# Fast matrix products for five instead of four pairs in the second GEMM of an H3 + feed-forward kernel, with the factors of w2 made earlier and kept in DRAM

## The chip, the core and the metric

The kernel runs on one NeuronCore of a Trainium2 chip. The metric is the device time of one execution in microseconds (us), as the median of several runs. Engines: PE multiplies matrices, DVE (VectorE) and ACT (ScalarE) work element by element, POOL (GpSimd) here mostly issues DMAs, SP (SyncE) issues the other DMAs. Each engine runs its instructions in program order; they wait for each other by semaphores.

## The reference

x is [2048, 1024] (S by D), w1 [1024, 3584], w2 [3584, 1024] (D by F, F by D), all float32.

```python
xn = _layernorm(x, axis=-1)
return x + _A_ref(xn, A_k, A_v, A_shift_k, A_ssm_k, A_ssm_D) + _B_ref(xn, B_w1, B_w2)

def _A_ref(q, k, v, shift_k, ssm_k, ssm_D):   # H3
...
    kv = k_shift * v                          # k_shift: causal convolution of k, 4 taps
...
    y = irfft(rfft(kv, 2*S) * rfft(ssm_k, 2*S))[:S] + kv * ssm_D
    return q * y

def _B_ref(x, w1, w2):                        # feed-forward
    h = jnp.einsum("bsd,df->bsf", x, w1)
    h = _silu(h)
    return jnp.einsum("bsf,fd->bsd", h, w2)
```

(The two transforms along S are written shorter here.)

## The kernel before

Every matrix product is made of float16 pieces: a float32 operand is split into a high and a low half, and three matmuls (high by high, high by low, low by high) are summed in PSUM. A split is one ACT instruction (high) and one DVE scalar_tensor_tensor (low). Matmuls have 128x128 weights and as a rule 512 columns.

Stages, in the order of PE. **GEMM1** (`units()`, L1085; matmuls at L1027 to L1029) makes the activations h = silu(xn·w1), in 28 pairs i of two blocks j of 128 columns of F; much of it by seven products in the manner of Strassen (P1, P7, P6, P2, P5, P3, P4) instead of eight. The activations go to DRAM, `hs`. **GEMM2** (`feed_forward()`, L1134; matmuls at L1179 to L1181 in `steps2`) has two parts. The plain part runs over two halves of the columns of D (h), 16 row blocks (t) and five chunks (c) of four j: 20 of the 28 j. Then `units2()` (L1197) does the other eight j, the pairs in `PAIRS`, by the seven products, in eight units u of 7 products with one step per pair. For these pairs `quad` (L908) combines activations right after GEMM1's unit and stores them to DRAM, `hsfS` and `hsfA`. The w2 factors of the seven products (sums and differences of w2's quarters, split in halves) are made at the end of `norms_w2()` (L1388), from raw w2 loaded again, straight into SBUF, when the plain part frees the places for them. Split w2 chunks and these factors lie in eight large SBUF places (`x` tiles; `W2PLACE`, `FPLACE`).

Beside the GEMMs runs the **convolution** (`convolution()`, L1499), in eight groups of four t each: stage 1 of the transform on PE (L1668 to L1670), evacuated as `tmp` by DVE or `spec` by ACT, a pointwise part in `spec` on DVE and ACT, the inverse on PE (L1861 to L1863) from the split `zh`/`zl`, and `yt`, a DVE scalar_tensor_tensor that reads PSUM and is added to `out` in DRAM by POOL's DMAs. Stage 1 and inverse matmuls stand between the GEMMs' matmuls.

h tiles are loaded by `load_h()` (L1345) on SP, one DMA per tile (`wo<-hs`, and `wo<-hsfS`/`wo<-hsfA` for the products), into a ring of 12 halves of the six `wo` buffers. A half is free again after its last matmul, which sets how far ahead loads can go.

What sets the order: the kernel's Python program has a planner (`Order`, L107). Every part is a generator that yields operations; each engine's next instruction is the one whose estimated start less its stream's bias is smallest. Costs per operation are formulas (`V` for DVE, L320; `A` for ACT, L323; `T` for PE), biases are given with `add`. So a changed number moves instructions on every engine. All DVE tensor_tensor instructions are issued at L348, scalar_tensor_tensor at L351, ACT at L359, SP's DMAs at L332, transposing ones at L341, POOL's at L345.

Of the kernel before, what the change touches and what calls it, by code (L numbers as in the profile page):

```python
# [20 lines left out]
P = 128  # L21
# [9 lines left out]
W = 512  # L31
# [20 lines left out]
RAWS = {"B11": [(0, 0)], "B21": [(1, 0)], "B22": [(1, 1)], "T1": [(0, 1), (0, 0)], "T2": [(0, 0)],  # L52
        "T3": [(1, 1), (0, 1)], "T4": [(1, 0)]}
# [197 lines left out]

class Parts:
# [43 lines left out]
def h3_ffn_kernel(ctx, tc, x, kp, vs, fs, shift, dskip, w1, w2, cfwd, cinv, out):  # L296
# [53 lines left out]
    def v_stt(o, a, s, b, op0, op1, **k):  # L350
        return V(lambda: nc.vector.scalar_tensor_tensor(o, a, s, b, op0=op0, op1=op1), o,  # L351
                 [a, b] + ([] if isinstance(s, float) else [s]), **k)

    def a_act(o, i, func, scale=1.0, bias=None, total=None):
# [8 lines left out]
        p.busy += 0.07 * (len(ins) - 1) - 0.06 * (i.space == bass.MemoryType.PSUM)  # L363
        if total is not None:
            p.busy += 0.19
            p.writes.append(total)
# [11 lines left out]
    hsf = [{p[0]: dram.tile([4, P, NQ, 2, P], F16, name=f"hsf{p[0]}{b}") for p in PRODUCTS.values()} for b in range(2)]  # L378
# [111 lines left out]
    def norm_act(ring, ss, ns, then, flags, margin=1.5, joined=False):  # L490
# [15 lines left out]
        yield V(chain, e, [sums], us=0.33)  # L506
# [293 lines left out]
    def scales_w1():  # L800
        for n, (_, i) in enumerate(pairs):
            yield (0.25, 0.2, 0.1, 0.05)[min(n, 3)]
# [105 lines left out]
    def quad(i, sp):  # L908

        def factors(names, hf, toks=()):  # L910
# [4 lines left out]
            for f, name in enumerate(names):  # L915
                yield L(hsf[sp][name][:, :, PAIRS.index(i)].rearrange("q p h s -> p q (h s)"),
                        ht[:, 4 * f:4 * f + 4].rearrange("p q h s -> p q (h s)"))
                ttok.set()
# [103 lines left out]
    def steps(o, w, xf, first, last, more=False):  # L1022

        for k in range(KH):
# [5 lines left out]
            yield T(mm, o, [w[:, :, k], xf[:, :, k]], 3 * (size(o) / 2400 + 0.003))  # L1030
# [54 lines left out]
    def units():  # L1085
# [5 lines left out]
        for n, (i, sp) in enumerate(todo):  # L1091
# [3 lines left out]
            if i in PAIRS:  # L1095
                add(quad(i, sp), 0.1)
# [37 lines left out]
    def feed_forward():  # L1134
# [12 lines left out]
        for h in range(2):  # L1147
            for ts in TOGETHER[h]:
                pos = {}
                for c in range(NC):  # L1150
                    for t in ts:
# [7 lines left out]
                        yield from steps2(pos[t][0], hx, wc, c == 0, c == NC - 1)  # L1159
# [3 lines left out]
                        if c == NC - 1:  # L1163
                            add(result(h, t, *pos[t]), EB)
                            if h == 0:
                                flag["result", t].set()
        flag["last part"].set()
# [6 lines left out]
    def steps2(po, hx, wc, first, last, more=False, of=range(4), q=slice(0, W)):  # L1174
        o = po[:, q]
        for n in of:
            def mm(n=n):
                kw = dict(skip_group_check=more)
                nc.tensor.matmul(o, hx[:, n, 0, :], wc[:, n, 0, q], start=first and n == 0, stop=False, **kw)  # L1179
                nc.tensor.matmul(o, hx[:, n, 0, :], wc[:, n, 1, q], start=False, stop=False, **kw)  # L1180
                nc.tensor.matmul(o, hx[:, n, 1, :], wc[:, n, 0, q], start=False, stop=last and n == 3, **kw)  # L1181
            yield T(mm, o, [hx[:, n], wc[:, n, :, q]], 3 * (size(o) / 2400 + 0.005))
# [14 lines left out]
    def units2():  # L1197

        def product2(n, u, o, first=False, of=range(4), q=slice(0, W)):
# [4 lines left out]
            yield from steps2(o, hx, wc, first, True, not first, of, q)  # L1204
            if 3 not in of or q.stop < W:
                return
            htok.set()
            if u == len(tiles2) - 1:
# [5 lines left out]
        for u in range(len(tiles2)):  # L1214
# [18 lines left out]
            if last:  # L1233
                yield from product2("P2", u, one[0], of=(0, 1))
# [6 lines left out]
            if last:  # L1241
                yield from product2("P2", u, one[0], of=(2, 3))
# [102 lines left out]
    def load_h():  # L1345
        yield flag["factors"]
        for h in range(2):
            for c, t in [(c, t) for ts in TOGETHER[h] for c in range(NC) for t in ts]:
                yield wo.ready
                flag["h", h, t, c].what = o, _ = wo.tile([P, 4, 2, P], F16)  # L1350
                yield L(o, hs[t // 4][t % 4][:, PLAIN[4 * c]:PLAIN[4 * c] + 4])
                flag["h", h, t, c].set()
        for u, n in uses2():
            sp, q = tiles2[u]
            yield wo.ready
            flag["h2", u, n].what = o, _ = wo.tile([P, NQ, 2, P], F16)
            yield L(o, hsf[sp][PRODUCTS[n][0]][q])
            flag["h2", u, n].set()
        flag["h end"].set()
# [28 lines left out]
    def norms_w2():  # L1388
# [17 lines left out]
        add(load_w2(), 0.05)  # L1406
        for h in range(2):
            for c in range(NC):
# [5 lines left out]
                flag["w2", h, c].n = 2  # L1414
                for a in (0, 2):
                    i = PLAIN[4 * c + a] // 2
                    raw, tok = yield from next_w2()
                    add(split(wc[:, a:a + 2, 0, :], wc[:, a:a + 2, 1, :], raw, tau[:, i:i + 1], (tok, flag["w2", h, c])), 0.05)
        yield places[FPLACE[0]].ready
        hold, ktok = places[FPLACE[0]].tile([P, NQ, W], F32)  # L1420
        for k, (name, (_, of)) in enumerate(PRODUCTS.items()):
            r = places[FPLACE[k + 1]]
            yield r.ready
            wc, wtok = w2f[name] = r.tile([P, NQ, 2, W], F16)
            flag["w2f", name].n = NQ
            held = of in ("T2", "T3", "T4")
            if held:
                if of != "T3":
                    yield flag["held", before]
                flag["held", of].n = NQ  # L1430
                before = of
            for a, i in enumerate(PAIRS):
                raw, tok = yield from next_w2()
                src, toks = raw, (tok, flag["w2f", name])
                if held:
                    src, toks = hold[:, a], (flag["w2f", name], flag["held", of])
                if of == "T3":
                    b12, t12 = yield from next_w2()
# [566 lines left out]
```

## Time and profile before

| | |
|---|---|
| time of 3 runs, median (lowest to highest) | 1239.55 us (1238.06 to 1240.69) |
| span of the profiled execution | 1235.0 us (its own total time is not recorded) |
| busy: PE, DVE, ACT, POOL | 1225.7, 1121.9, 744.0, 142.0 us |
| DMA traffic | 293.21 MB, mean 237 GB/s |

The page gives busy time per engine, then a chain of work that ended last; the views of the trace add waits (who waited for whom, total us, times, longest), groups by line and shape (busy us, mean ns), windows (busy us and count per engine in a stretch) and a timeline. A mean in a group is the time from an instruction's start to its end; neighbours on an engine overlap a little, so that starts can lie closer.

GEMM1's last matmul starts at 580.8 us, the last load for the plain part of GEMM2 is issued at 1033.4 us, and the last matmul of all starts at 1230.3 us.

### The profile page before, as it was taken

Reading aid. Unit: us, or ns where it says so; the run is one execution under the profiler, and the core shown is the slowest. Engines: PE = TensorE matmul, PEld = TensorE weight load, DVE = VectorE, ACT = ScalarE, POOL = GpSimd, SP = SyncE. Lnnn points to the kernel's source line nnn. Section 1 sums busy time; section 2 is a strip of 40 time slices with the busy share of each in tenths; the row PEclk is TensorE's granted clock in tenths of the full one; section 3 lists DMA queues with packets and bytes.
Section 4 is the critical chain, followed back from the end, with each engine's and each line's share of the span. In section 5 each row is a group of like instructions: output and inputs, shape, how many; then the busy total and the mean of one; then the engine's idle time right before and its main releaser. Section 6 shows DMA issues by size and latency. Waiting matters only on the chain.

```text
span 1235.0 us, 17269 instructions
## 1 busy us (share of the span) xinstructions
PE 1225.7 (99%) x6128; PEld 596.6 (48%) x6128; DVE 1121.9 (91%) x1366; ACT 744.0 (60%) x1299; POOL 142.0 (12%) x164
## 2 busy tenths in 40 slices
PE   9999999999999999999999999999999999999998
PEld 7645444444444444444444544544454454445445
DVE  8999996989699979998999899989979979998993
ACT  7778887877767787758653632563263264536231
POOL 2000000000000020001110300210030030113114
PEclk9999999999999999999999999999999999999999
DMA  9289889999999698968997887699596688978777
GB/s 341 78 278 312 304 298 308 286 273 335 324 359 286 218 303 278 268 213 242 345 336 184 190 257 179 155 271 259 115 216 171 134 167 247 255 161 137 164 147 103
DMA packets 254438, 293.21 MB, mean 237 GB/s; under 512 B 48784, under 2 KB 167824, under 8 KB 252176
## 3 DMA queue, kind: packets, MB, share of 16 engines
q1 hardware_dynamic: 227760, 267.46, 69.3%
q0 software_dynamic: 26592, 24.65, 15.1%
q8 instruction: 48, 0.79, 0.3%
q14 instruction: 38, 0.31, 0.1%
HBM read 193.48 MB, written 98.57 MB: 236 GB/s over the span
## 4 chain that ended last, share of the span: by engine, by line
PE 96%; DVE 2%; ACT 1%; issue 1%; DMA 1%; POOL 0%; DVEq 0%
PE ff L1179 15%; PE ff L1180 15%; PE ff L1181 15%; PE ff L1027 13%; PE ff L1028 13%; PE ff L1029 13%; PE ps L1668 2%; PE ps L1669 2%; PE ps L1670 2%; PE ft L616 1%; PE ps L1863 1%; PE ps L1861 1%; PE ps L1862 1%; DMA out<-yt 1%; PE ff L1932 1%
## 5 line engine op out<-in xcount | busy, mean ns | idle before, releaser
L1180 PE MATMUL ff<-x,wo 128*128 128x512 f16 (+2 forms) x872 | 328.5, 377 | 0.0
L1179 PE MATMUL ff<-x,wo 128*128 128x512 f16 (+2 forms) x872 | 328.4, 377 | 0.0
L1181 PE MATMUL ff<-x,wo 128*128 128x512 f16 (+2 forms) x872 | 328.4, 377 | 0.0
L1028 PE MATMUL ff<-x,wo 128*128 128x512 f16 (+2 forms) x840 | 306.7, 367 | 1.5 <-DVE x L351 1.5
L1027 PE MATMUL ff<-x,wo 128*128 128x512 f16 (+2 forms) x840 | 306.7, 367 | 0.2 <-ACT hf L359 0.2
L1029 PE MATMUL ff<-x,wo 128*128 128x512 f16 (+2 forms) x840 | 306.7, 367 | 0.1
L348 DVE TENSOR_TENSOR spec<-spec 128x1024 f32<-128x1024 f32 (+2 forms) x272 | 263.0, 999 | 2.4
L1181 PEld LDWEIGHTS <-wo 128*128 128x128 f16 x872 | 85.3, 98 | 101.5
L1179 PEld LDWEIGHTS <-wo 128*128 128x128 f16 x872 | 85.3, 98 | 100.7
L1180 PEld LDWEIGHTS <-wo 128*128 128x128 f16 x872 | 85.3, 98 | 99.4
L1029 PEld LDWEIGHTS <-wo 128*128 128x128 f16 x840 | 82.1, 98 | 92.3 <-issue 1.6
L1027 PEld LDWEIGHTS <-wo 128*128 128x128 f16 x840 | 82.1, 98 | 88.1
L1028 PEld LDWEIGHTS <-wo 128*128 128x128 f16 x840 | 82.1, 98 | 86.9 <-issue 0.5
L345 POOL DMA_DIRECT2D out<-hf x59 | 52.5, 890 | 445.0 <-ACT hf L359 341.8
L359 ACT ACTIVATE hf<-ff,invc 128x512 f32<-128x512 f32 x60 | 41.0, 684 | 101.4 <-PE ff L1181 81.8
L345 POOL DMA_DIRECT2D out<-yt x56 | 62.0, 1278 | 326.4 <-DVE yt L351 186.7
L348 DVE TENSOR_TENSOR tmp<-spec 128x2048 f32<-128x2048 f32 (+1 forms) x48 | 92.3, 1932 | 0.9
L351 DVE SCALAR_TENSOR_TENSOR ht<-hf,wsc,ht 128x1024 f16<-128x1024 f32 (+1 forms) x56 | 67.4, 1203 | 14.5 <-ACT ht L359 14.0
L351 DVE SCALAR_TENSOR_TENSOR acc<-kin,taps,acc 128x1024 f32<-128x1024 f32 x48 | 61.4, 1278 | 7.3 <-ACT acc L359 7.3
L359 ACT ACTIVATE spec<-ps 128x512 f32<-128x512 f32 x96 | 55.4, 591 | 19.9 <-PE ps L1670 18.6
L359 ACT ACTIVATE spec<-spec 128x1024 bf16<-128x1024 f32 x32 | 33.7, 1054 | 54.9 <-DVE spec L348 54.9
L351 DVE SCALAR_TENSOR_TENSOR wo<-raw,wsc,wo 128x512 f16<-128x512 f32 (+1 forms) x56 | 56.4, 1011 | 8.3 <-ACT wo L359 8.1
(183 smaller groups left out, 1751.1 us busy)
## 6 DMA issues: line engine op xcount, KB each, us to landing
wo<-hs SPq DMA_DIRECT2D x160, 256.0 KB, 3.6
hs<-ht SPq DMA_DIRECT2D x80, 256.0 KB, 4.5
wraw<-in_w SPq DMA_DIRECT2D x31, 512.0 KB, 5.4
out<-hf POOLq DMA_DIRECT2D x59, 256.0 KB, 4.5
raw<-in_w SPq DMA_DIRECT2D x28, 512.0 KB, 5.8
kin<-in_kp SPq DMA_DIRECT2D x16, 704.0 KB, 6.2
kf<-in_fs SPq DMA_DIRECT2D x8, 1024.0 KB, 5.9
hl<-in_vs SPq DMA_DIRECT2D x32, 256.0 KB, 6.1
```

Source lines behind the costliest of these rows:

```text
L345: return Op("POOL", 1.1, 4.8, lambda: nc.gpsimd.dma_start(o, i, accum_op=ADD), [i], [o], m, n)
L348: return V(lambda: nc.vector.tensor_tensor(o, a, b, op=op), o, [a, b], **k)
L351: return V(lambda: nc.vector.scalar_tensor_tensor(o, a, s, b, op0=op0, op1=op1), o, [a, b] + ([] if isinstance(s, float) else [s]), **k)
L359: nc.scalar.activation(o, i, func, scale=scale, **kw)
L1027: nc.tensor.matmul(o, w[:, 0, k], xf[:, :, k, 0], start=first and k == 0, stop=False, **kw)
L1028: nc.tensor.matmul(o, w[:, 0, k], xf[:, :, k, 1], start=False, stop=False, **kw)
L1029: nc.tensor.matmul(o, w[:, 1, k], xf[:, :, k, 0], start=False, stop=last and k == KH - 1, **kw)
L1179: nc.tensor.matmul(o, hx[:, n, 0, :], wc[:, n, 0, q], start=first and n == 0, stop=False, **kw)
L1180: nc.tensor.matmul(o, hx[:, n, 0, :], wc[:, n, 1, q], start=False, stop=False, **kw)
L1181: nc.tensor.matmul(o, hx[:, n, 1, :], wc[:, n, 0, q], start=False, stop=last and n == 3, **kw)
L1668: nc.tensor.matmul(o, cf[:, 0], hi[i], start=i == 0, stop=False, **kw)
L1669: nc.tensor.matmul(o, cf[:, 0], lo[i], start=False, stop=False, **kw)
```

## The change

The change has five parts. (1) Pair 7 joins the four pairs done by the seven products (`MORE`), so the plain part has 18 j in chunks of 4, 4, 4, 2 and 4. Its activations go to DRAM tensors of their own (`hsx`), four and three products to a tensor, and one load (`wo<-hsx`) brings a batch for a unit. (2) The factors of w2 are made by `factors_w2` while the plain part runs: each pair's raw rows are loaded once (two DMAs of 512 KB), split into a pair of `wo` halves lent for it (`Lent`), and stored to DRAM (`w2s`); `load_w2f` loads them into the places later, pair 7's apart (`HOMES`). Two more `wo` tiles go to these for good, so 7 halves stay for the h tiles. (3) `load_w2` waits for a flag before loading into places used a second time. (4) The planner's costs of DVE, ACT and PE operations are other numbers. (5) So are some biases.

```diff
-PAIRS = (8, 9, 12, 13)
-NQ = len(PAIRS)
-PLAIN = [j for j in range(NF) if j // 2 not in PAIRS]
-NC = len(PLAIN) // 4
+MAIN = (8, 9, 12, 13)
+MORE = (7,)
+PAIRS = MAIN + MORE
+NM, NE, NQ = len(MAIN), len(MORE), len(PAIRS)
+CHUNKS = [(0, 4), (4, 4), (8, 4), (12, 2), (20, 4)]
+NC = len(CHUNKS)
-FPLACE = (6, 3, 4, 0, 1, 5, 2, 7)
+FPLACE = (3, 4, 0, 1, 5, 2, 7)
+HOMES = ((6, 4), ("wo", 2), ("wo", 1))
...
-        return Op("DVE", us or 1.03 * (size(o) / 960 + 0.075), 0.16, f, ins, [o], m)
+        return Op("DVE", us or size(o) / 960 + 0.072, 0.16, f, ins, [o], m)
-        return Op("ACT", us or 1.02 * (0.16 + size(o) * 0.84e-3), 0.2, f, ins, [o], m)
+        return Op("ACT", us or 0.1 + size(o) / 1200, 0.2, f, ins, [o], m)
...
+        p.busy += 0.0 if isinstance(s, float) else 0.06
...
-            yield T(mm, o, [hx[:, n], wc[:, n, :, q]], 3 * (size(o) / 2400 + 0.005))
+            yield T(mm, o, [hx, wc[:, :, q]], 3 * (size(o) / 2400 + 0.0024))
...
     def load_h():
         yield flag["factors"]
+        yield wo.pairs
+        whole, _ = wo.pair([P, 2 * W])
+        ctxs["stage"] = Lent([whole])
+        for where, n in HOMES:
+            if where == "wo":
+                yield wo.ready if n * NE == 1 else wo.pairs
+                t, _ = (wo.tile if n * NE == 1 else wo.pair)([P, n, NE, 2, W], F16)
+                lent.append(t)
...
             yield L(o, hsf[sp][PRODUCTS[n][0]][q])
             flag["h2", u, n].set()
+            k, f = BATCH[n]
+            if f == 0:
+                m = min(NX, 7 - NX * k)
+                yield wo.ready
+                o, tok = wo.tile([P, NX, NE, 2, P], F16, m)
+                flag["h2x", u, k].what = o, tok
+                yield L(o[:, 0:m], hsx[sp][k][q])
+                flag["h2x", u, k].set()
...
+    def factors_w2():
...
+        def factors(names, src, i, tok):
+            n = len(names)
+            stage = ctxs["stage"]
+            yield stage.ready if n == 1 else stage.pairs
+            o, otok = (stage.tile if n == 1 else stage.pair)([P, n, 2, W], F16, n)
+            yield from split(o[:, :, 0], o[:, :, 1], src, tau2[:, i:i + 1], (tok,))
+            for f, name in enumerate(names):
+                n = product_of[name]
+                yield L(w2s[n][:, PAIRS.index(i)], o[:, f])
+                otok.set()
+                flag["w2s", n].set()
+
+        for i in PAIRS:
...
+                yield L(r, w2r[:, 2 * i + q].rearrange("p (h w) -> p h w", h=2))
...
+            yield from factors(("B21", "B22"), low, i, ltok)
+            yield v_tt(low[:, 1], low[:, 1], top[:, 1], SUB)
+            yield v_tt(top[:, 1], top[:, 1], top[:, 0], SUB)
+            yield from factors(("B11", "T1"), top, i, ttok)
+            yield v_tt(top[:, 0], low[:, 1], top[:, 0], ADD)
+            yield v_tt(low[:, 0], low[:, 0], top[:, 0], SUB)
+            add(factors(("T4", "T3"), low, i, ltok), SB)
+            add(factors(("T2",), top[:, 0:1], i, ttok), SB)
...
+    def load_w2f():
...
+        for k, name in enumerate(PRODUCTS):
+            yield flag["w2s", name]
+            r = places[FPLACE[k]]
+            yield lambda: r.ready() and flag["w2 last", FPLACE[k]]()
+            wc, wtok = w2f[name] = r.tile([P, NM, 2, W], F16)
+            yield L(wc, w2s[name][:, 0:NM])
+            flag["w2f", name].set()
+            if not left:
+                left = yield from home(*homes.pop(0))
+            w2x[name] = left.pop(0)
+            yield L(w2x[name], w2s[name][:, NM:])
...
-        for gen, bias in ((loads(), 0.05), (load_v(), 0.04), (gate(), 0.04), (signal_parts(), CB), (parts_of(), CB), (stage1(), 0.02),
-                          (transforms(), 0.02), (squares_w2(), 0.0), (rest(floor), 0.0)):
+        for gen, bias in ((loads(), 0.05), (load_v(), 0.14), (gate(), 0.04), (signal_parts(), CB), (parts_of(), CB), (stage1(), 0.02),
+                          (transforms(), 0.0), (squares_w2(), 0.0), (rest(floor), 0.0)):
...
-    add(spill_w1(), 0.0)
+    add(spill_w1(), 0.2)
...
-    add(load_h(), 0.05)
+    add(load_h(), 0.3)
```

How instructions move is best seen in three places. The first is DVE in the plain part of GEMM2, at the last two yt of the convolution's group 3 (line L351 before is L364 of the change, L348 is L361). Before:

```order
L351 SCALAR_TENSOR_TENSOR zl1_6998<-spec_2120,csc1_5560,zh1_6997 128x1024
L348 TENSOR_TENSOR tmp_6880<-tmp_6880,ps2_6881 128x2x256
L348 TENSOR_TENSOR tmp_6880<-tmp_6880,ps3_6885 128x2x256
L351 SCALAR_TENSOR_TENSOR hl0_2121<-kf_6275,csc0_6397,hl0_2121 128x512
L351 SCALAR_TENSOR_TENSOR yt0_3150<-ps1_6999,csc1_5560,ht1_200 128x512
L351 SCALAR_TENSOR_TENSOR zl0_7045<-spec_2120,csc1_5560,zh0_7044 128x1024
L348 TENSOR_TENSOR tmp_6880<-tmp_6880,ps0_7019 128x2x256
L351 SCALAR_TENSOR_TENSOR yt0_3150<-ps3_7043,csc1_5560,ht1_200 128x512
```

The change, at the same yt:

```order
L364 SCALAR_TENSOR_TENSOR zl1_7243<-spec_2184,csc1_5505,zh1_7242 128x1024
L361 TENSOR_TENSOR spec_2184<-spec_2184 128x2x512
L364 SCALAR_TENSOR_TENSOR wo0_201<-wraw0_3215,tau2_166,wo0_201 128x2x512
L361 TENSOR_TENSOR tmp_7088<-tmp_7088,ps3_7089 128x2x256
L361 TENSOR_TENSOR tmp_7088<-tmp_7088,ps0_7093 128x2x256
L361 TENSOR_TENSOR wraw0_3215<-hf1_208,wraw0_3215 128x512
L361 TENSOR_TENSOR hf1_208<-hf1_208,wraw0_3215 128x512
L364 SCALAR_TENSOR_TENSOR hl1_2186<-kf_6390,csc0_6513,hl1_2186 128x512
L364 SCALAR_TENSOR_TENSOR yt0_3214<-ps2_7244,csc1_5505,ht1_211 128x512
L364 SCALAR_TENSOR_TENSOR zl0_7304<-spec_2184,csc1_5505,zh0_7303 128x1024
```

Between the same parts of the convolution now stand splits of w2 factors (into `wo0_201`, the lent buffer) and the sums of raw quarters (`wraw`, `hf`) that make them.

The second place is SP's queue in the plain part, late, where the first two factors (products P1 and P7) are stored for the last pair and loaded back:

```order
L345 DMA wo_202<-hs_84 128x512
L354 DMA_TRANSPOSE hl_2186<-cm 128x8x128
L345 DMA w2sP_77<-wo_201 128x1024
L345 DMA w2sP_81<-wo_201 128x1024
L345 DMA x_7293<-w2sP_77 128x4096
L345 DMA x_7307<-w2sP_77 128x1024
L345 DMA kf<-in_fs 128x2048
L345 DMA ht_211<-in_x 128x2x128 x2
L345 DMA w2sP_83<-wo_201 128x1024
L345 DMA w2sP_78<-wo_201 128x1024
L345 DMA x_7392<-w2sP_78 128x4096
L345 DMA x_7307<-w2sP_78 128x1024
```

None of these stores and reloads exists before; each reload waits for the store just ahead of it, and the h loads (`wo<-hs`) stand behind it in the queue. The 128x512 load is the chunk of two j.

The third place is the end of SP's queue. Before:

```order
L332 DMA wo_193<-hsfA_69 128x1024
L332 DMA wo_190<-hsfS_70 128x1024
L332 DMA wo_190<-hsfS_71 128x1024
L332 DMA wo_191<-hsfA_72 128x1024
L332 DMA hf_197<-out 128x512 x2
L332 DMA out<-hf_197 128x512
```

The change:

```order
L345 DMA wo_202<-hsfA_69 128x1024
L345 DMA wo_202<-hsfS_70 128x1024
L345 DMA hf_209<-out 128x512 x2
L345 DMA wo_204<-hsx_76 128x768
L345 DMA wo_205<-hsfS_71 128x1024
L345 DMA wo_206<-hsfA_72 128x1024
L345 DMA out<-hf_209 128x512
```

The load of `out`, which waits for the convolution's last yt to be added, was behind all h loads and now stands ahead of three.

More of the change, by code (lines that the diff above doesn't have):

```diff
@@ L249, in pair, with __init__ @@
         return shaped(self.taken(k), shape, dt), token
+class Lent(Halves):
+    def __init__(self, whole):
+        self.whole = whole
+        self.held = [[None, None] for _ in whole]
+        self.age = [0] * len(whole)
+        self.count = 0
 class Parts:
```

177 lines of the change are left out of this document (98 added, 79 removed).

## The prediction

> **What bounds the kernel now.** I read the page first: the busy shares, then the chain that ended last.
>
> ```profile
> span 1235.0 us, 17269 instructions
> ...
> PE 1225.7 (99%) x6128; PEld 596.6 (48%) x6128; DVE 1121.9 (91%) x1366; ACT 744.0 (60%) x1299; POOL 142.0 (12%) x164
> ...
> PE 96%; DVE 2%; ACT 1%; issue 1%; DMA 1%; POOL 0%; DVEq 0%
> ```
>
> PE is busy for 99% of the span and is 96% of the chain, so a matmul that goes is a matmul's time won, as long as what feeds PE keeps up. Next, the waits of PE over the whole run:
>
> ```profile
> PE ff L1028 <- DVE x L351: 1.5, 1, 1.5
> PE ps L1668 <- DVE yt L351: 1.4, 1, 1.4
> PE ff L1932 <- DVE oneb L402: 1.1, 1, 1.1
> PE ps L1668 <- DVE tmp L348: 0.5, 1, 0.5
> PE ff L1027 <- ACT hf L359: 0.2, 1, 0.2
> ```
>
> The 1.5 and 1.1 belong to the first 20 us, which the change leaves alone. The other three are 2.1 us, all between 569 and 588 us, where GEMM1 ends. Two of them are waits for DVE, the second engine at 91%. So the third view is that of windows, over the end of GEMM1 and the plain part of GEMM2 (busy us and instructions of PE, PEld, DVE, ACT, POOL; clock; DMA share; GB/s):
>
> ```profile
> 550.00:600.00 50.00, 47.88 (x245) 23.75 (x243) 45.66 (x52) 37.96 (x53) 7.57 (x8) 1.00 0.91 253
> 600.00:650.00 50.00, 50.00 (x234) 22.70 (x233) 49.79 (x50) 28.94 (x55) 5.59 (x6) 1.00 1.06 342
> 650.00:700.00 50.00, 50.00 (x258) 24.99 (x257) 48.00 (x54) 24.82 (x47) 7.42 (x8) 1.00 0.79 189
> 700.00:750.00 50.00, 50.00 (x235) 22.66 (x233) 45.18 (x47) 22.23 (x49) 8.33 (x9) 1.00 0.88 229
> 750.00:800.00 50.00, 50.00 (x257) 24.90 (x256) 46.17 (x53) 20.21 (x37) 7.38 (x8) 1.00 0.72 163
> 800.00:850.00 50.00, 50.00 (x233) 22.63 (x233) 45.59 (x52) 29.54 (x57) 7.49 (x8) 1.00 0.98 277
> ```
>
> PE has no gap from 600 us on, and DVE idles 0.2 + 2.0 + 4.8 + 3.8 + 4.4 = 15.2 us of these last 250. This idle time is the room into which the change puts work.
>
> **Fewer matmuls.** The plain part has 18 j instead of 20: 2 j × 16 t × 2 halves × 3 matmuls = 192 fewer. The products have five pairs instead of four: 8 units × 7 products × 1 pair × 3 = 168 more. Net 24 fewer; the program order confirms it, 866 instead of 872 on each of GEMM2's lines plus the same narrow pieces at the end. What one costs is its distance to the next, not its 379 ns:
>
> ```profile
> 1150.12 0.38 PE L1180 MATMUL ff<-x,wo 128*128 128x512 f16 x1
> ...
> 1166.09 0.38 PE L1179 MATMUL ff<-x,wo 128*128 128x512 f16 x1
> ```
>
> These two starts are 74 matmuls apart: 15.97 / 74 = 0.216 us. 24 × 0.2156 = **5.17 us** less PE work. Nothing else on PE changes in amount.
>
> **More work on DVE and ACT, at another time.** The rows that price it:
>
> ```profile
> L351 DVE SCALAR_TENSOR_TENSOR ht<-hf,wsc,ht 128x1024 f16<-128x1024 f32 x48 | 61.4, 1279 | 10.9 <-ACT ht L359 10.4 <-DMA kin<-in_kp 0.3
> L348 DVE TENSOR_TENSOR hf<-ff,hf 128x512 f32<-128x512 f32 x52 | 35.6, 684 | 3.7 <-PE ff L1029 3.7
> L351 DVE SCALAR_TENSOR_TENSOR x<-x,tau,x 128x512 f16<-128x512 f32 x12 | 8.8, 742 | 0.0
> L359 ACT ACTIVATE ht<-hf,wsc 128x1024 f16<-128x1024 f32 x48 | 54.9, 1145 | 1.2 <-DVE hf L348 0.2
> L359 ACT ACTIVATE x<-x,tau 128x512 f16<-128x512 f32 x12 | 8.5, 719 | 19.1 <-DVE x L348 19.1
> ```
>
> Pair 7's activations add 2 splits of 1024, 2 of 512 and 8 sums of 512; the w2 factors go from 20 splits of 1024, 28 of 512 and 16 sums to 33, 5 and 20. Together +15 × 1.279 − 21 × 0.742 + 12 × 0.684 = +11.8 us on DVE and +15 × 1.145 − 21 × 0.719 = +2.1 us on ACT. ACT, busy at 60%, hides its share. DVE goes to about 1133.7 of some 1230 us, still not the bound of the run; but the work now stands between about 600 and 800 us, and the burst after 1000 us shrinks.
>
> For that stretch I sum DVE's work in program order against PE's. A row's own duration is too long for this, since neighbours overlap:
>
> ```profile
> 569.44 1.28 DVE L351 SCALAR_TENSOR_TENSOR x<-wraw,tau,x 128x1024 f16<-128x1024 f32 x1
> 570.64 1.28 DVE L351 SCALAR_TENSOR_TENSOR ht<-x,wsc,ht 128x1024 f16<-128x1024 f32 x1
> 571.84 0.69 DVE L348 TENSOR_TENSOR hf<-ff,hf 128x512 f32<-128x512 f32 x1
> ```
>
> Two 1.28 us splits start 1.20 us apart; 512-wide sums likewise cost 0.60 to 0.65, 512-wide splits 0.665. From GEMM1's end to the last yt of the convolution's group 3 (its fourth), before has 219 DVE instructions, 206.9 us, against 216.4 us of matmuls. Of the change I count 42 more: 17 splits of 1024 (20.4 us), 20 sums of 512 (12.4), four spec sums of 1024 (4.7), and small ones: 245.4 us against 234.5 us of matmuls. DVE falls behind PE. The place that decides is shortly ahead: a yt that frees PSUM for a stage-1 matmul has 236.9 us of DVE work before it and 234.5 on PE's side, a wait of 2.4 us near 810 us. I checked the method on before: there the same sum's only shortfall is 0.56 us, at a stage-1 matmul, and the trace has this at that place:
>
> ```profile
> 569.58 0.38 PE L1668 MATMUL ps<-hl,cfw 128*128 128x512 f16 x1 [0.54 <-DVE tmp L348]
> ```
>
> On before the sum runs 0.6% longer than the trace, so of the 2.4 us I take off 1.4 and keep 1.0. The other shortfalls of the change, at matmul positions 228, 411, 552 and 898 us, are 0.1, 0.7, 1.1 and 1.5 us, with the same correction 0.1, 0.1, 0.4 and 0.1. Before lost 2.1 us in three waits where its sum has 0.56, so I add 0.6 us of hand-over for each of the last three places (552, 810, 898), and 0.7 us for late loads (next part): 1.7 + 1.8 + 0.7 = **4.2 us** of stalls past the start. The bounds: 0, if DVE always runs ahead of its order, and the full idle time of the windows (rival C).
>
> **Shorter load distance.** The lent wo pair and the places for w2's pair 7 leave 7 halves instead of 12 for the h tiles. Loads are then issued 54 to 72 matmuls ahead (11.6 to 15.5 us; 45, 9.7 us, at the least, in the products) instead of some 130 (28 us). Rows on what a load takes, in 560 to 620 us, in 620 to 622, and in the products (count, size, median us to landing):
>
> ```profile
> wo<-hs SPq DMA_DIRECT2D x18, 256.0 KB, 6.5
> ...
> wo<-hs SPq DMA_DIRECT2D x1, 256.0 KB, 9.8
> ...
> wo<-hsfS SPq DMA_DIRECT2D x32, 256.0 KB, 3.3
> ```
>
> In the products 9.7 against 3.3 is safe. At 580 to 640 us, with 342 GB/s and a DMA share of 1.06, the longest landing leaves 11.6 − 9.8 = 1.8 us for SP's own issuing; I take 0.7 us of loss in all, between 0 and rival D. The 18 MB of factor stores and reloads run after 625 us, where the windows have 163 to 277 GB/s. In two places SP's queue holds a reload behind the store just issued; the h loads queued behind it, and through them PE, have about 9 us left there, against a landing of 3 to 5.
>
> Two small edits cost nothing. Stage 1's PSUM halves get 9 other matmuls in between (1.94 us) instead of 12, and ACT's copy needs 0.59:
>
> ```profile
> L359 ACT ACTIVATE spec<-ps 128x512 f32<-128x512 f32 x96 | 55.4, 591 | 19.9 <-PE ps L1670 18.6
> ```
>
> At the end the hf<-out load, which in before sits on SP until the last yt is out, now stands ahead of the last three wo loads:
>
> ```profile
> 1194.57 21.64 SPq L332 DMA_DIRECT2D hf<-out  x2
> ...
> 1215.60 0.74 DVE L351 SCALAR_TENSOR_TENSOR wo<-ps,csc,ht 128x512 f32<-128x512 f32 x1
> ...
> 1228.69 2.67 SPq L332 DMA_DIRECT2D out<-hf  x3
> ```
>
> That would starve PE if the yt came as late as 1215.6; but the change has the fourth t's yt ahead of the last unit's sums, so SP should be free some 20 us before the end, and the first of the three loads is needed 9 us before it: 6 us to spare after its landing. The tail behind the last matmul stays.
>
> **The sum.** The profiled span of 1235.0 us lies 4.55 us under the median of 1239.55; I carry that over. 1239.55 − 5.17 − 2.1 (stalls that were) + 4.2 (stalls to come) = **1236.5 us**. Within 0.2% (2.5 us) is what a measurement here can't tell from no change: faster means below 1237.1, slower above 1242.0.
>
> **The rivals.**
> - **B, given back.** DVE keeps a third of its 15.2 us of idle time, 5.1, in the stretch to 810 us, because part of it is waits inside one chain: 1236.5 + 5.1 − 2.4 (what the freed order still absorbs between 810 and 898) = 1239.2. For it: the waits of DVE in 600 to 810 us, below, are mostly for ACT. Against it: a DVE that is late finds its inputs ready.
> - **C, DVE becomes the bound.** All of the idle time up to 810 us stays, 0.2 + 2.0 + 4.8 + 3.8 + about 0.9 = 11.7 us; stage 1 at 810 us then waits for yt by 11.7 + 1.0: 1239.55 − 5.17 − 2.1 + 12.7 = 1245.0. It decides from 8.8 us of kept idle time on (slower), 6.3 breaks even.
>
> ```profile
> DVE spec L348 <- ACT spec L359: 4.7, 4, 3.5
> DVE acc L351 <- ACT acc L359: 3.3, 1, 3.3
> DVE tmp L348 <- ACT spec L359: 2.0, 4, 0.6
> ```
>
> - **D, the ring of 7 halves starves PE** at 580 to 640 us. If a load takes longer than its 11.6 us from freed half to landed tile, each turn of the ring (about 11 us) loses the excess, some 6 turns there: 1.5 us too long (11.6 of landing and 1.5 of issuing) costs 9 us, 1236.5 − 0.7 + 9 = 1244.8. For it: 9.8 us landings. Against: the median of 6.5.
> [...]
>
> **How the numbers follow.** Forecast 0.48 (faster, 1233.6 to 1237.1), B 0.31 and E 0.02 (within 0.2%), C 0.10 and D 0.09 (slower). So faster 0.48, same 0.33, slower 0.19. The range leaves out the better part of C and D (0.15) and, below, 0.04 for a run that loses no time at all (1239.55 − 5.17 − 2.1 = 1232.3): 1233.6 to 1243.
>
> **What would show it.** PE's busy time falls by about 5 us, and 24 matmuls are gone from GEMM2's lines. DVE is busy for over 49 of 50 us in each window from 600 to 800 us, with its waits for ACT spec nearly gone there. PE's waits name DVE yt or tmp at a stage-1 line near 800 us, below 2 us each. Waits of PE for wo<-hs at 580 to 640 us would be D; gaps of DVE beside a waiting PE at 750 to 810 us would be C; a last wait for hsx or hsf in the final 10 us would show the end misjudged. The prediction is wrong if GEMM2's loads or stores, rather than DVE, turn up in PE's waits.

## The result, and the profile after

The change makes the kernel slower: a median of 1245.0 us (1243.2 to 1246.5, 5 runs) against 1238.1 us of before in the same comparison (1236.7 to 1240.7). The ratio is 1.0059 with a 95% interval of 1.0048 to 1.0070, so 6 to 9 us. The forecast was 1236.5, which is 3.1 below the 1239.55 that it started from; the measured time is 6.9 above before's.

The page after (busy time and share of the span by engine):

```profile
span 1241.4 us, 17337 instructions
...
PE 1223.3 (99%) x6110; PEld 594.0 (48%) x6110; DVE 1131.0 (91%) x1372; ACT 741.7 (60%) x1293; POOL 143.5 (12%) x164
```

The matmul instructions are 18 fewer: 30 of 512 columns are gone, and six pairs of 384 and 128 columns have come, which together is the work of 24 whole ones. DVE has 9.1 us more (11.8 were counted), ACT 2.3 us less (2.1 more were counted). So PE has 5.2 us less to do, yet the span is 6.4 us longer. (PE's busy time falls by 2.4 us only: a matmul is recorded with 0.38 us and the next starts 0.216 us later if nothing holds it, so the first 0.16 us of a wait count as busy.) The windows over the end of GEMM1 and the plain part, columns as before:

```profile
550.00:600.00 50.00, 48.65 (x249) 24.12 (x248) 43.28 (x58) 37.78 (x57) 9.64 (x9) 1.00 0.82 219
600.00:650.00 50.00, 49.15 (x230) 22.22 (x229) 49.83 (x50) 30.89 (x56) 3.46 (x4) 1.00 1.08 333
650.00:700.00 50.00, 49.59 (x232) 22.39 (x231) 49.41 (x56) 19.24 (x32) 3.48 (x4) 1.00 0.92 266
700.00:750.00 50.00, 49.12 (x252) 24.47 (x251) 44.72 (x50) 28.14 (x52) 12.30 (x12) 1.00 1.03 281
750.00:800.00 50.00, 48.80 (x228) 21.99 (x227) 49.59 (x53) 21.64 (x40) 3.47 (x4) 1.00 0.86 246
800.00:850.00 50.00, 47.89 (x245) 23.73 (x243) 49.16 (x58) 27.45 (x45) 12.25 (x12) 1.00 0.96 276
```

PE, which had no gap from 600 us on, now idles in each of these windows. DVE is full as forecast, but for one window: 700 to 750, with 5.3 us idle. The waits of PE in the whole run, the larger ones:

```profile
PE ps L1761 <- ACT tmp L374: 2.5, 3, 1.9
PE ff L1205 <- ACT hf L374: 2.0, 1, 2.0
PE ft L635 <- DVE xt L616: 1.6, 2, 1.2
PE ff L1051 <- DVE x L364: 1.5, 1, 1.5
PE ps L483 <- ACT spec L374: 1.2, 1, 1.2
...
PE ps L1761 <- DVE spec L361: 1.0, 1, 1.0
PE ps L1761 <- ACT spec L374: 0.9, 1, 0.9
PE ff L1206 <- DVE x L364: 0.8, 1, 0.8
```

Small waits are hidden in the overlap of matmuls, so I also took the start of every matmul and subtracted the distance that the one before it needs (0.2157 us for 512 columns). What is left over is time that PE lost. By stretches of the run, in us:

| | to 150 | 150 to 550 | 550 to 600 | 600 to 850 | 850 to end | sum |
|---|---|---|---|---|---|---|
| before | 6.6 | 0.0 | 2.6 | 0.3 | 0.1 | 9.6 |
| after | 8.9 | 2.3 | 1.8 | 7.0 | 2.6 | 22.6 |
| few_rows (below) | 8.0 | 2.2 | 0.8 | 0.5 | 0.2 | 11.7 |
| before_few (below) | 6.6 | 0.0 | 1.3 | 0.2 | 0.0 | 8.1 |

13.0 us more lost, 5.2 saved, and 1.4 less behind the last matmul make the 6.4 us. Over half of the loss is in 600 to 850 us.

What emptied DVE in 700 to 750 us is in its waits for its own yt. In the whole run of before, then of after (us in all, how often, the longest):

```profile
DVE yt L351 <- DMA out<-yt: 1.3, 2, 0.7
```

```profile
DVE yt L364 <- DMA out<-yt: 10.6, 10, 3.5
```

A yt can be written only when the DMA that adds the last one in its half of the buffer to `out` has landed. The two longest cases after, in the timelines of POOL (which issues these DMAs) and DVE:

```profile
706.07 2.20 POOL L358 DMA_DIRECT2D out<-yt  x2 [4.12 <-DVE yt L364]
709.13 1.10 POOL L358 DMA_DIRECT2D out<-yt  x1 [0.86 <-DVE yt L364]
715.10 1.09 POOL L358 DMA_DIRECT2D out<-yt  x1 [4.87 <-issue]
```

```profile
715.69 0.75 DVE L364 SCALAR_TENSOR_TENSOR yt<-ff,csc,ht 128x512 f32<-128x512 f32 x1 [1.09 <-DMA out<-yt]
716.91 0.69 DVE L361 TENSOR_TENSOR spec<-spec,ps 128x512 f32<-128x512 f32 x1 [0.47 <-ACT spec L374]
721.15 0.75 DVE L364 SCALAR_TENSOR_TENSOR yt<-ps,csc,ht 128x512 f32<-128x512 f32 x1 [3.55 <-DMA out<-yt]
```

Their times from issue to landing, median of the three issued in 705 to 711 us:

```profile
out<-yt POOLq DMA_DIRECT2D x3, 128.0 KB, 8.8
```

The longer wait has a second part. Two DMAs empty one half of the buffer, and the fourth of this group is issued only at 715.10 us, after POOL has stood still for 4.87 us with no wait that the profile names. It starts 0.26 us after the first of the three before it has landed, and its own 6.0 us then release the yt at 721.15. Before has the same pause, only shorter:

```profile
698.49 1.10 POOL L345 DMA_DIRECT2D out<-yt  x1 [2.70 <-issue]
```

In the 17 traces in which these DMAs (out<-yt and out<-ht) carry 128 KB, never more than three of them are under way at once. In 115 cases POOL stands still in this way for over 0.8 us ahead of one, with three under way, and issues it 0.25 to 0.36 us after the first of the three has landed.

DVE stands still for 4.6 us in the one stretch in which it has nothing to spare. Up to 830 us it never catches up, and PE loses about as much at the next places where it waits for a convolution step: 1.0 us at 716, 1.4 at 798, 2.1 at 817. The last of these is named ACT tmp: ACT's queue had a `zh` in front, which waited 3.6 us for a spec of the late DVE.

### The profile page after: what moved, and what is told of

Its sections match the earlier page's. It is cut to its first block, busy times and chain, and to the rows that moved or that the text cites. A ratio compares the mean times of both kernels' runs of the same rounds, so it can differ in the third digit from the quotient of the medians.

```text
span 1241.4 us, 17337 instructions
## 1 busy us (share of the span) xinstructions
PE 1223.3 (99%) x6110; PEld 594.0 (48%) x6110; DVE 1131.0 (91%) x1372; ACT 741.7 (60%) x1293; POOL 143.5 (12%) x164
## 5 line engine op out<-in xcount | busy, mean ns | idle before, releaser
L1205 PE MATMUL ff<-x,wo 128*128 128x512 f16 (+1 forms) x841 | 316.4, 377 | 2.0 <-ACT hf L374 2.0
L1206 PE MATMUL ff<-x,wo 128*128 128x512 f16 (+1 forms) x841 | 316.4, 377 | 0.8 <-DVE x L364 0.8
L1207 PE MATMUL ff<-x,wo 128*128 128x512 f16 (+1 forms) x841 | 316.4, 377 | 0.0
L1051 PE MATMUL ff<-x,wo 128*128 128x512 f16 (+2 forms) x840 | 306.8, 367 | 1.5 <-DVE x L364 1.5
L1052 PE MATMUL ff<-x,wo 128*128 128x512 f16 (+2 forms) x840 | 306.9, 367 | 0.5 <-DVE wo L364 0.4
L1050 PE MATMUL ff<-x,wo 128*128 128x512 f16 (+2 forms) x840 | 306.8, 367 | 0.6 <-DVE hf L361 0.4
L361 DVE TENSOR_TENSOR spec<-spec 128x1024 f32<-128x1024 f32 (+2 forms) x272 | 263.8, 1000 | 2.3
L358 POOL DMA_DIRECT2D out<-yt x62 | 69.6, 1318 | 372.1 <-DVE yt L364 337.8
L361 DVE TENSOR_TENSOR tmp<-spec 128x2048 f32<-128x2048 f32 (+1 forms) x48 | 92.4, 1933 | 0.8
L364 DVE SCALAR_TENSOR_TENSOR ht<-hf,wsc,ht 128x1024 f16<-128x1024 f32 (+1 forms) x56 | 66.3, 1183 | 3.9 <-ACT ht L374 3.9
L374 ACT ACTIVATE ht<-hf,wsc 128x1024 f16<-128x1024 f32 (+1 forms) x56 | 59.9, 1070 | 9.8 <-DVE hf L361 3.9
L364 DVE SCALAR_TENSOR_TENSOR wo<-raw,wsc,wo 128x512 f16<-128x512 f32 (+1 forms) x56 | 56.2, 1012 | 7.0 <-ACT wo L374 6.8
L364 DVE SCALAR_TENSOR_TENSOR acc<-kin,taps,acc 128x1024 f32<-128x1024 f32 x48 | 61.4, 1279 | 1.1 <-ACT acc L374 1.1
```

Source lines behind the costliest of these rows:

```text
L358: return Op("POOL", 1.1, 4.8, lambda: nc.gpsimd.dma_start(o, i, accum_op=ADD), [i], [o], m, n)
L361: return V(lambda: nc.vector.tensor_tensor(o, a, b, op=op), o, [a, b], **k)
L364: p = V(lambda: nc.vector.scalar_tensor_tensor(o, a, s, b, op0=op0, op1=op1), o, [a, b] + ([] if isinstance(s, float) else [s]), **k)
L374: nc.scalar.activation(o, i, func, scale=scale, **kw)
L1050: nc.tensor.matmul(o, w[:, 0, k], xf[:, :, k, 0], start=first and k == 0, stop=False, **kw)
L1051: nc.tensor.matmul(o, w[:, 0, k], xf[:, :, k, 1], start=False, stop=False, **kw)
```

## The experiments

Times are medians; the ratio is to the kernel before in the same comparison, with its 95% interval. All 18 runs are here. "Order held" means that each engine's sequence of instructions is that of the kernel it is made from.

**1. Less DVE work in the stretch, order held (small_sums).**

```diff
-            yield v_tt(low[:, 1], low[:, 1], top[:, 1], SUB)
+            yield v_tt(low[:, 1], low[:, 1], top[:, 1], SUB, n=8)
...
```

> The kernel after the change, every engine's order held, but the 20 sums that make the w2 factors (512 columns, about 0.60 us of DVE each) work on 8 columns: about 11 us less DVE work between 620 and 820 us; the factors' values are left wrong by that. Theory S (DVE, filled with factor work, sets PE's pace between 600 and 850 us): PE's lost time in 600 to 850 us falls from 7.0 us to 2 or less, time 1239 to 1241. Rival N (the new numbers of the planner made a worse order everywhere): the order is the same, so nearly the same losses, 1243 to 1245. Rival R (the ring of 7 halves): no change, 1244 to 1245.

Measured: 1240.3 us (1237.3 to 1244.6), ratio 1.0018 (1.0006 to 1.0031). 4.7 us less than after, about as theory S said. But DVE still waited 3.0 us for out<-yt in 600 to 850 us, and PE lost 4.1 us there, more than S allowed (the profiled run, of 1243.2 us, lies 2.9 above the median). 11 us less work didn't buy 11 us.

**2. The numbers of the planner alone, on the kernel before (numbers_alone), and the rest of the change with the old numbers (old_numbers).** The edit of the first is the costs and biases of the diff above; the second is the change without them.

> The kernel before, with only the planner's costs and biases of the change. Theory S: PE loses under 1 us in 600 to 850 us; the time lies between that of before (1238) and 1242.5, according to how much of the 2.1 us lost at the start and the 2.3 us lost in GEMM1 comes from the numbers. Rival N: PE loses 3 us or more in 575 to 850 us too, and the time is above 1243. Rival R: like before, 1238.

> The kernel after the change with the planner's costs and biases of before. Theory S: PE still loses 5 us or more in 600 to 850 us; time 1238 to 1246 (1238.1 - 5.2 + 6.8 = 1239.7 if start and GEMM1 lose nothing, more if the old costs fit DVE worse). Rival N: the saving shows, 1233 to 1236. Rival R: 1240 or more, with PE's waits for h loads.

Measured: numbers_alone 1250.7 us (1247.8 to 1251.9), ratio 1.0098 (1.0081 to 1.0114); old_numbers 1241.8 us (1238.3 to 1247.2), ratio 1.0029 (1.0014 to 1.0043). Rival N had its first half: with no matmul saved and no factor made elsewhere, the new numbers cost 12.6 us, spread over 575 to 625, 780, 890 and 1105 us. Its second half fell: without them the change still is slower, as S said, though PE lost 4.1 us in 600 to 850 us in that trace and not the 5 of S. In the profiled run of old_numbers one wait stands out, in GEMM1:

```profile
234.52 0.38 PE L1050 MATMUL ff<-x,wo 128*128 128x512 f16 x1
239.11 0.58 PE L1048 MATMUL ff<-x,wo 128*128 128x512 f16 x1 [4.21 <-DVE hf L361]
239.49 0.63 PE L1049 MATMUL ff<-x,wo 128*128 128x512 f16 x1
```

DVE had the sums and splits of pair 7's activations ahead of an evacuation. What follows on PE is in the last section.

**3. Without pair 7 (four_pairs, new numbers; four_old, old numbers).**

```diff
-MORE = (7,)
+MORE = ()
-CHUNKS = [(0, 4), (4, 4), (8, 4), (12, 2), (20, 4)]
+CHUNKS = [(0, 4), (4, 4), (8, 4), (12, 4), (20, 4)]
...
```

> The change without pair 7: four pairs, 20 j in the plain part, w2 factors made ahead through DRAM (four fifths of the factor work), 10 halves left for h loads, new numbers. PE has 5.2 us more work than after the change. Theory S: 600 to 850 us still loses 3 to 6 us, time 1246 to 1249. Rival R: the loss in 600 to 850 us goes with the shorter ring, under 1.5 us, time 1241 to 1244. Rival N: like S, with the losses at start and in GEMM1 as after the change.

> The change without pair 7 and with the planner's costs and biases of before: only the making of the w2 factors ahead of time through DRAM is left, 10 halves for h loads. Theory F (moving the factors into 600 to 850 us costs by itself): PE loses 2.5 us or more there, 1239.5 to 1243. Rival P (it is pair 7): like before, 1236.5 to 1239.

Measured: four_pairs 1245.8 us (1243.4 to 1247.9), ratio 1.0061 (1.0042 to 1.0081); four_old 1245.1 us (1242.6 to 1245.6), ratio 1.0051 (1.0033 to 1.0069). Without pair 7, with either set of numbers and with 10 halves for the h loads, the kernel is as slow: rivals R and P fall. Four_old is even above F's range. PE loses 6.3 us in 600 to 850 us in both traces, but there DVE's waits for out<-yt are only 1.8 us (four_pairs) and 0.7 (four_old, of 5.3 in all), and 3.5 us of four_old's loss are waits of PE for DVE's zl. So these two orders lose by other waits than the change's. That making the factors ahead costs by itself isn't shown, as both are also new orders (theory O, below).

**4. Which numbers (dve_act_costs, pe_and_biases, on the kernel before).**

> The kernel before with the new costs of DVE and ACT in the planner, and nothing else of the change (PE's costs and all biases as before). Theory C (the new DVE and ACT costs make an order that meets PE too late in many places): as slow as with all numbers or slower, 1249 us or more. Rival B (a bias does it): within 1.5 us of before, 1237 to 1240.

> The complement of the last: the kernel before with the new PE costs and the new biases, DVE and ACT costs as before. Theory C: within 1.5 us of before, 1236.5 to 1239.5. Rival B: 1247 us or more.

Measured: dve_act_costs 1258.1 us (1256.3 to 1259.3), ratio 1.0163 (1.0149 to 1.0178); pe_and_biases 1242.8 us (1240.3 to 1243.4), ratio 1.0037 (1.0023 to 1.0051). The DVE and ACT costs alone do more harm than all numbers together. But the other half is not harmless either, against theory C. So "the new costs are bad" was too simple, and I formed theory O: the time hangs on the particular order.

**5. One number by half a per cent (dve_1025, dve_1031), and by one per cent on the change (after_101).**

```diff
-        return Op("DVE", us or 1.03 * (size(o) / 960 + 0.075), 0.16, f, ins, [o], m)
+        return Op("DVE", us or 1.025 * (size(o) / 960 + 0.075), 0.16, f, ins, [o], m)
```

> The kernel before with one number changed by half a per cent: the factor of the planner's DVE cost is 1.025 instead of 1.03. Theory O (the time hangs on the particular order, and any new order of this planner loses some us): slower by 3 us or more, 1240 to 1246. Theory C (only costs well below the old ones lose): within 1.5 us of before, 1236 to 1239.

> As the last, with 1.031. Theory O: differs from before by more than 1.5 us, either way. Theory C: within 1.5 us of before.

> The change with one number moved by one per cent: the planner's DVE cost times 1.01. Theory O (each new order lands somewhere in a band of several us): off the change's 1245 by more than 1.5 us, either way, between 1238 and 1252, with losses at other places. Theory C: within 1.5 us of 1245.

Measured: dve_1025 1246.6 us (1245.2 to 1252.0), ratio 1.0078 (1.0054 to 1.0103); dve_1031 1239.8 us (1237.4 to 1242.0), ratio 1.0016 (1.0007 to 1.0025); after_101 1249.0 us (1247.5 to 1249.7), ratio to before 1.0085 (1.0070 to 1.0101), 4 us above the change. Theory O holds in all three (dve_1025 even lies 0.6 us above the range written for it). Half a per cent in one cost is worth 9 us, more than the whole effect of the change, by waits that before doesn't have. PE's largest ones in dve_1025:

```profile
PE ff L1180 <- DVE x L351: 2.9, 1, 2.9
PE ff L1027 <- ACT hf L359: 2.2, 1, 2.2
```

Behind each of these two, seven or eight matmuls start at half rate (last section), which costs 1.5 to 1.7 us more.

Every order made here, with all of its work in place, is slower than the one of before. That says that before's order is a good draw; it doesn't say what a good draw has.

**6. Other orders for the change (old_dve_act, quad_first, best).** The first takes the change with before's DVE and ACT costs. The second is old_numbers with one bias, the third has two more:

```diff
-                add(quad(i, sp), 0.1)
+                add(quad(i, sp), 0.3 if i in MORE else 0.1)
...
-    SB = 0.05
+    SB = 0.2
```

> The change with the DVE and ACT costs of before in the planner; the structure, PE's new costs and the new biases stay. Theory C: it is 3 us or more faster than the change, 1236 to 1242. Theory O: no rule; it need not be faster, 1238 to 1248, with losses at other places.

> The change with the planner's costs and biases of before, and one bias more: the stream that combines pair 7's activations gets 0.3 (0.1 for the other pairs). Theory Q (with the old numbers, eight sums and splits of pair 7 ahead of an evacuation make PE wait 4.4 us at 239 us, and the half clock behind it costs another 1.5): both go, 5 to 6 us less than with the old numbers, 1235 to 1237. Rival: the same DVE work makes PE wait elsewhere in GEMM1 or GEMM2, 1239 or more.

> As the last, with the bias of the convolution's transforms at 0.0 (as in the change) and of the w2 factors at 0.2 instead of 0.05 (they are taken earlier). If theory S is only a matter of order (the factor work fits between 600 and 850 us), PE loses under 2.5 us there and the time is 1232 to 1236, faster than before. If the stretch is too full for any order (S as predicted), it loses 4 us or more there and the time is 1237 or more.

Measured: old_dve_act 1245.8 us (1243.7 to 1247.1), ratio 1.0064 (1.0047 to 1.0080), no faster than the change: O, not C. quad_first 1239.6 us (1236.2 to 1243.1), ratio 1.0019 (1.0010 to 1.0028): the wait at 239 us is gone and it is 2.2 us faster than old_numbers, but PE waits at other places, as the rival said. best 1243.6 us (1240.1 to 1247.2), ratio 1.0048 (1.0031 to 1.0064): a miss, with 4.0 us lost in 600 to 850 us, the second of the two cases written. DVE's waits for out<-yt in its trace are 8.7 us, in quad_first's 1.7.

**7. Lighter DMAs for yt, order held (few_rows, small_few, before_few).**

```diff
-                yield G(out4[b][:, :, t, g * P:(g + 1) * P], yt[:, b])
+                yield G(out4[b][:, :, t, g * P:(g + 1) * P], yt[:, b], rows=16)
```

> The kernel after the change, every engine's order held, with the 20 sums of the w2 factors on 8 columns (as in small_sums) and the DMAs that add yt to out moving 16 of 128 partitions: the factors' values and most of the convolution's share of the output are left out. Theory S with the wait for out<-yt as part of it (DVE waits 4.6 us for out<-yt in 700 to 750 us, 3.5 in one piece): the wait of PE at 716 us goes, PE loses under 1.5 us between 620 and 850 us, and the time is 2 us or more below small_sums, 1236 to 1238.5. Rival: the wait at 716 us stays at 2 us (it comes from ACT or from the order alone), 1239.5 to 1241.

> The kernel after the change, order held, with the DMAs that add yt to out moving 16 of 128 partitions (most of the convolution's share of the output is left out); the factors' sums are whole. Theory S-sum (in 600 to 850 us DVE's amount of work decides): PE still loses 3 us or more there, 1239 to 1242. Theory S-yt (its waits for out<-yt decide): under 2 us, 1235 to 1238.

> Control: the kernel before, order held, with the same small DMAs for yt (most of the convolution's share of the output is left out). If these DMAs cost every order the same, it gains as much as the change does by them (about 5 to 8 us); if they hurt only where DVE has no room, it gains under 2.5 us, 1235.5 to 1237.5.

Measured: few_rows 1232.3 us (1231.7 to 1232.4), ratio 0.9951 (0.9936 to 0.9966); small_few, with the small sums too, 1232.7 us (1232.3 to 1233.4), ratio 0.9959 (0.9944 to 0.9974); before_few 1236.7 us (1235.2 to 1237.9), ratio 0.9987 (0.9978 to 0.9996). These runs settle it for the change's order. With all of DVE's work in place, the lighter DMAs take 12.7 us off the change and 1.5 off the kernel before, and the smaller sums then add nothing. Under these DMAs the change is 4.4 us faster than before, nearly the whole saving of 5.2. Both few_rows and small_few are about 3 us faster than the theory of the yt waits said, since losses go outside of 600 to 850 us too (the table above). few_rows in windows:

```profile
650.00:700.00 50.00, 50.00 (x243) 23.53 (x242) 49.55 (x56) 21.12 (x37) 3.46 (x4) 1.00 0.91 252
700.00:750.00 50.00, 50.00 (x249) 24.08 (x247) 49.55 (x53) 28.62 (x54) 9.82 (x12) 1.00 0.98 306
750.00:800.00 50.00, 50.00 (x235) 22.64 (x233) 49.62 (x58) 21.40 (x36) 3.49 (x4) 1.00 0.91 240
800.00:850.00 50.00, 49.92 (x256) 24.86 (x255) 49.13 (x54) 29.56 (x50) 9.86 (x12) 1.00 0.89 262
```

DVE is busy 49.1 to 49.6 of 50 us, and PE has no gap. As the order is the same, I set the starts of the 1372 DVE instructions of after and few_rows side by side. In 540 to 870 us after falls behind only at six of them: at 581 us (a yt, 1.0 us), 587 and 591 (spec, 1.3 together), 716 (a yt, 1.2), 717 (spec, 0.6) and 721 (a yt, 3.6). Every other one keeps its distance to 0.3 us, so nothing is slower, DVE only stands. The same two yt in few_rows:

```profile
710.93 0.74 DVE L364 SCALAR_TENSOR_TENSOR yt<-ff,csc,ht 128x512 f32<-128x512 f32 x1
711.59 0.67 DVE L361 TENSOR_TENSOR spec<-spec,ps 128x512 f32<-128x512 f32 x1
712.19 0.74 DVE L364 SCALAR_TENSOR_TENSOR yt<-ps,csc,ht 128x512 f32<-128x512 f32 x1
```

The lighter DMAs shorten both parts of a yt's wait: they land sooner (4.4 us at the median instead of 6.5), and up to five are under way at once. They also leave 7.3 MB to the others (wo<-hs lands in 3.7 us instead of 4.4), which may have helped at 587 to 609 us. This run doesn't part these three.

**8. The planner told of the landing time (late_best, before_late).**

```diff
-        return Op("POOL", 1.1, 4.8, lambda: nc.gpsimd.dma_start(o, i, accum_op=ADD), [i], [o], m, n)
+        return Op("POOL", 1.1, 7.5, lambda: nc.gpsimd.dma_start(o, i, accum_op=ADD), [i], [o], m, n)
```

> As the run best, with one number more: the planner takes 7.5 us instead of 4.8 from the issue of an adding DMA (out<-yt) to its landing, near what the traces show (6.5 us median, 8.6 at 706 us). Theory Y (the losses of the new orders come from a yt that is placed before the last DMA from its buffer has landed, with DVE full behind it): DVE's waits for out<-yt fall from 8.7 us to under 2, and the time is 1231 to 1236, faster than before. Theory O alone (any order lands in a band): 1237 to 1250, with or without those waits.

> The kernel before with the same number at 6.0 instead of 4.8, nothing else. Theory Y: DVE's waits for out<-yt go, and the time is that of before_few or a little above, 1236 to 1238.5. Theory O alone: off before's time by more than 1.5 us.

Measured: late_best 1246.3 us (1241.1 to 1247.1), ratio 1.0071 (1.0057 to 1.0085); before_late, with 6.0, 1242.1 us (1240.9 to 1242.5), ratio 1.0031 (1.0019 to 1.0043). Two misses. In late_best the waits for out<-yt fall from 8.7 to 2.5 us, as meant, but the new order loses 2.0 us at 236, 2.3 at 582 and 4.6 at 818 to 836. In before_late 1.1 of the 1.3 us of these waits stay, and the time is off before's by 4.4 us, as theory O said. So another order that has few of those waits is not enough: every new order is a new draw. (The traces of quad_first, best and late_best are of runs 3.4 to 5.2 us faster than their medians, so they don't show all that these orders lose.) No version that keeps all the work beat the kernel before.

## Why the prediction was wrong

- **The matmuls saved** (5.17 us): right. PE's work, summed by the same distances, is 5.2 us less, and few_rows against before_few shows 4.4 us of it in the time. Only "the same narrow pieces" was misread: there are more of them, so the instructions are 18 fewer and not 24.
- **DVE's sum in 575 to 810 us** (245.4 us against 234.5, and near 810 us a wait of 1.0 us with 0.6 of hand-over): somewhat too high, but no more. few_rows has all of this work in the same order, and PE loses 0.5 us in the whole of 600 to 850. After the change DVE is full, at 49.8, 49.4 and 49.6 us of 50 in three of the four windows from 600 to 800 us, as forecast, and its waits for ACT spec in 600 to 810 us are down from 6.7 us to 0.5.
- **The stalls past the start (4.2 us)**: this is the step that failed. 13.7 us were lost after the first 150 us. The sum contained DVE's durations and PE's, but no DMA that DVE waits for. That a yt needs the landing of an earlier one's DMA stood in the trace of before with 1.3 us, all of it in the 600 to 810 us that the sum is about, and I took it for nothing. After the change these waits are 10.6 us, 4.6 of them where DVE had no room; PE's waits behind it then name ACT's tmp and spec, not DVE's yt or tmp as forecast. The yt there don't follow each other sooner: the fourth of its group could have started 12.6 us after the first (705.0 to 717.6), and in before's group it starts 11.2 us after it (690.9 to 702.1) without a wait. The DMAs are slower, 8.8 us instead of 6.2 for the first, so the fourth is issued later and lands 15.1 us after the first was issued, instead of 10.0. Beside them 281 GB/s move in 698 to 716 us, and 177 in 686 to 702 us of before; that this traffic, with the factors' stores and loads in it, slows them is likely, but no run shows it. With the yt's DMAs light, 3.7 us are lost after the first 150, close to the 4.2 of the sum, but in part by luck: 2.2 of them lie in GEMM1, where the sum has 0.2.
- **The start and GEMM1** (start "left alone", 0.2 us in 150 to 450): wrong by 2.3 and about 2 us. The new numbers move instructions from the first microseconds on; numbers_alone, without any of the rest, loses 0.8 us more than before by 150 us and 1.9 in 150 to 550. Of the start a part is scatter (few_rows, same order: 8.0 instead of 8.9).
- **The load distance**: no PE wait for wo<-hs anywhere. Rival D fell, and the 7 halves cost nothing.
- **The end** ("costs nothing"): wrong by 2.0 us and by a mechanism that I didn't list (the tail behind the last matmul, said to stay, is 1.4 us shorter). SP is free early, as said, but ACT's last but two evacuation waited for a staging tile until a POOL DMA had landed, and PE for it. POOL issues this DMA behind yt's, and in few_rows the wait is gone.

```profile
1225.78 0.69 ACT L374 ACTIVATE hf<-ff,invc 128x512 f32<-128x512 f32 x1 [10.93 <-DMA out<-hf]
```

- **Rival C's price** (1245.0) is what was measured, but by coincidence and not by its mechanism. DVE's old idle time did not stay; it went, and a new wait of another kind came. For the same reason rival B's condition, old idle time that stays, did not come either, and the price of B (1239.2) is too low. **Rival E**, a lower granted clock behind a long wait of PE, did not come: PE's clock is 1.00 in all six windows shown above, and its longest waits, of 1.9 and 2.0 us, are not followed by a lower one (1.00 in 817.4 to 820 and in 1226.4 to 1229.5 us). The run of before, with no wait of PE over 1.5 us, shows no such drop either; what the other runs show of it is in the last section.
- **The planner's new numbers**: the sum gives them no term of their own. They alone make the kernel before 12.6 us slower, those of DVE and ACT alone 20.9. Of the change's 6.9 us I can't say how much is the order's draw and how much the factor work, since no run has the one without the other: what is shown is that in the change's own order the loss goes when yt's DMAs are light.

## What to carry to other kernels

When work is moved to fill an engine's idle time, add up not only its busy time: list each wait of that engine for a DMA, however small before, because an engine without room hands them on (here DVE stood for 4.6 us, and PE lost 4.5 at the next places), and look what sets when that DMA is issued. Where a list planner makes the order, a change of its numbers is a change of the whole program: test it alone, and draw a few neighbouring values to see how wide the band is before reading a meaning into one result. An experiment that keeps every order and makes one suspected operation small tells causes apart that a new order only mixes.

## What the runs showed that I had not expected

One eighth of the bytes doesn't make an adding DMA eight times faster. Median landing in the run after and in few_rows:

```profile
out<-yt POOLq DMA_DIRECT2D x62, 128.0 KB, 6.5
```

```profile
out<-yt POOLq DMA_DIRECT2D x62, 16.0 KB, 4.4
```

The small ones also go with steadier times of the change: few_rows spreads over 0.7 us in 4 runs, after over 3.2 in 5. before_few still spreads over 2.7 us in 10.

The second surprise is POOL's pause: three adding DMAs of 128 KB under way at once, and no fourth in any trace, while of those of 16 KB up to five are.

The clock: after old_numbers' wait of 4.2 us at 239 us, seven matmuls start 0.38 to 0.43 us apart instead of 0.216, about half rate. Windows of PE around it (busy, clock):

```profile
225.00:239.10 14.10, 9.90 (x47) 4.43 (x46) 14.00 (x21) 12.85 (x24) 0.00 (x0) 0.99 0.93 298
239.00:243.00 4.00, 3.89 (x12) 1.46 (x12) 3.65 (x5) 2.66 (x5) 0.00 (x0) 0.61 1.07 348
243.00:246.00 3.00, 3.00 (x16) 1.35 (x15) 2.58 (x4) 2.12 (x4) 0.00 (x0) 1.00 0.58 176
```

The granted clock averages 0.61 over these 4 us, the half rate lasts about 3 us, and PE loses 1.5 us more. It also comes after shorter waits. In dve_1031 a wait of 2.07 us is followed by eight matmuls 0.37 to 0.43 us apart:

```profile
1081.53 0.59 PE L1179 MATMUL ff<-x,wo 128*128 128x512 f16 x1 [2.07 <-ACT hf L359]
```

```profile
1081.00:1085.00 4.00, 3.47 (x9) 1.27 (x9) 4.00 (x5) 0.47 (x1) 0.88 (x1) 0.57 0.53 115
```

In late_best a wait of 2.41 us is followed by full clock:

```profile
817.59 0.38 PE L1759 MATMUL ps<-hl,cfw 128*128 128x512 f16 x1 [2.41 <-ACT tmp L372]
```

```profile
817.50:821.00 3.50, 3.41 (x20) 1.91 (x20) 3.50 (x4) 3.04 (x7) 0.00 (x0) 1.00 0.93 301
```

Over all 20 traces, after their first 30 us, none of PE's 20 waits of 1.3 to 1.9 us is followed by half rate, 6 of the 12 of 2.0 to 2.4 us are, and all 7 of 2.9 to 5.1 us. So 13 of the 19 waits of 2.0 us or more were paid for twice, by the wait and by the matmuls behind it. What parts the 6 of 2.0 to 2.4 us from the other 6, no run shows.
